# A linear-attention recurrence with MoE attention: input A without its zeros, loads one at a time, keys behind y

## The chip, the core and the metric

The kernel runs on one core of a Trainium2 chip. The metric is the device time of one execution in microseconds (us). The core's engines work through queues of their own in program order and wait for each other by semaphores: PE (TensorE: matmuls and transposes by matmul, into PSUM), DVE (VectorE), ACT (ScalarE), POOL (GpSimd) and SP, whose queue here does nothing but issue DMA loads and stores. PEld is PE's loading of weights.

## The reference, cut to what matters

```python
def _attn_ref(r, k, v, w, a, b):          # 4 batches, 8 heads, 768 steps, 40 wide
    for t in range(S):
        y[:, :, t] = np.einsum('bhd,bhde->bhe', rt, state)
        Sa = np.einsum('bhde,bhe->bhd', state, at)
        state_decay = state * wt[:, :, None, :] - np.einsum('bhd,bhe->bhde', Sa, bt)
        state = state_decay + np.einsum('bhd,bhe->bhde', vt, kt)
...
def _moe_ref(x, w_gate, wq, wk, wv, wo):  # x is y, as 4 x 768 x 320; 4 experts, the best 2 per token
        a = softmax of scale * (x @ wq[e]) @ (x @ wk[e]).T, causal
        out += weight of expert e * (a @ (x @ wv[e]) @ wo[e])
```

The recurrence over 768 steps comes first; its output y is the input of the mixture of attention experts. All is float32.

## The kernel before

**Tiling.** The 32 batch-heads are two halves s of 16, on partitions 0 to 39 and 64 to 103. The 768 steps are cut into 24 chunks of 32 steps, and the chunks into 6 windows W of 4. Within a chunk the recurrence is solved by matmuls: a triangular system is inverted once for each window (`invert`, sides P and Q on PE, fourteen elimination steps "t" on DVE), and the state ST is carried from chunk to chunk.

**Preparation of a window** (`prep`, two halves a = 0, 1 of the steps' columns, written "0x" or "1x"). Letters: w loads decay EW (into EW0), l loads EK (into KB, keys and b), e loads EA (into AB; each head's columns stand with zeros for the other half, 320 KB for one partition group). f and g are range flags on ACT, written to a scrap tile JK. a and s are scans over EW on DVE (SUF and SC), b a copy and a reciprocal between them (PC, D1P). X or x multiplies AB in place by SC (POOL or DVE, two instructions), K and H multiply the two halves of KB by SUF on POOL (two instructions each), p does K's part on DVE. m0 and m1 (`mm`) are 32 matmuls each into PSUM tile PK, read out by DVE as GB and GK and spread by POOL.

**The main loop** (24 + 1 turns n) walks the list MAIN. In a turn, each step belongs to chunk n, n-1 or n+1: g (state times AB, ACT evicts GT), f of chunk n-1 (into PF; DVE masks it to FX), t (transposed state, ACT evicts SD), k = keys of chunk n+1 (eight transposes into PK, ACT evicts LS), u (the solve, ACT evicts R), y of chunk n-1 (needs FX, SD and LS), z (DVE scales y to XT; every second chunk stores it to xT), s (state update; DVE adds it to the next ST), w (transpose of R, ACT evicts VR), v of chunk n+1. At the last chunk of a window, y's place also issues q, the gauge (rescaling by PC) of the state, and s has a gauge of its PSUM result.

**Chunk loads** are tied to steps: v loads V1 of chunk n+2, w loads R2 (VX) of n+1, y loads RX, f loads RB.

**Side work** is placed by hand: SIDE gives for each window the jobs of turns -3 to 3 relative to its first chunk (turn 4(W-1)), separated by "/" into places 0 to 9; a place k stands right behind the k-th step of MAIN. Window 1 has SIDE1 and AHEAD, window 0 has START. L258 is the DVE addition that ends side Q; it reads PK and finishes the inverse TT that u needs. Engines take all this in program order, so what stands in the list behind a waiting instruction waits with it.

**After the loop** the MoE part runs; `prepare` hangs its first loads and splits behind places 3, 5 and 7 of turns 21 to 23.

Of the kernel before, what the change touches and what calls it, by code (L numbers as in the profile page):

```python
# [21 lines left out]
NW, NC = 6, 24  # L22

SIDE = {
    -3: "0w/////0f",
    -2: "///0l1l//0g////0a0b0K0H",
    -1: "0e1e/0s0X1w///////1a1b1p",
    0: "1s1H1X////m0/1f1g////m1L",
    1: "/t14////B///t14",
    2: "/T////////P",  # L30
    3: "/////D////Q",
}
START = "x0 0w 0l 0e 1w 1l 1e x1 c0 0a 0b 0f 0g 0k 0s 0x 1a 1b 1f 1g m0 1k 1s 1x x2 m1 L B k0 t28 T D"
AHEAD = "0w 0l 1l 0e 1e 0a 0b 0f 0g 0s 0K 0H 0X 1w"

SIDE1 = {
    0: "1a1b1K1H//1s1X//m0/1f1g",
    1: "////m1/L/t4//t14",
    2: "/t10T/////B",
    3: "////P/D////Q",  # L40
}


def layouts(r, k, v, w, a, b):

    f = np.float32
    con = np.ascontiguousarray
    def em(x):
        x = x.reshape(2, 2, 8, 6, 4, 32, 40)
        return x.transpose(3, 1, 0, 6, 2, 4, 5)  # L50
    w33 = np.ones((6, 2, 2, 40, 8, 4, 33), f)
    w33[..., 1:] = em(w)
    w33[..., 0, 0] = 0
    EA = np.zeros((6, 2, 2, 40, 32, 2, 32), f)
    for s in range(2):
        EA[:, :, s, :, :, s] = em(a)[:, :, s].reshape(6, 2, 40, 32, 32)
    EK = np.stack([em(b), em(k)], 6)
    EK = EK.reshape(6, 2, 2, 40, 4, 2, 4, 2, 32).transpose(0, 1, 2, 3, 4, 6, 5, 7, 8)
    def ch(x):
        return x.reshape(2, 8, 2, 24, 32, 40)  # L60
    rr, vv = ch(r), ch(v)
    return {"EW": w33.reshape(6, 2, 2, 40, 1056), "EA": EA.reshape(6, 2, 2, 40, 2048), "EK": con(EK).reshape(6, 2, 2, 40, 2048),
            "V1": con(vv.transpose(3, 2, 0, 4, 1, 5)).reshape(24, 128, 320), "VX": con(vv.transpose(3, 2, 4, 1, 0, 5)).reshape(24, 2, 32, 640),
            "RB": con(rr.transpose(3, 0, 5, 1, 2, 4)).reshape(24, 2, 40, 512), "RX": con(rr.transpose(3, 2, 5, 1, 0, 4)).reshape(24, 2, 40, 512)}

# [17 lines left out]
def recurrence(tc, ctx, I, xT, FL, CM, early, tail=None):  # L83
    nc = tc.nc
    ep = early.enter_context(tc.tile_pool(name="early", bufs=1, side="right"))
    sp = ctx.enter_context(tc.tile_pool(name="rec", bufs=1))
    pp = ctx.enter_context(tc.tile_pool(name="rps", bufs=1, space=PSUM))
    V, A, T, PL, SY = nc.vector, nc.scalar, nc.tensor, nc.gpsimd, nc.sync
# [17 lines left out]
    O1 = MT[:, 0:512].rearrange("p (n t) -> p n t", n=32)  # L106
    DD = ring("DD", [128, 32, 16], 1, ep)[0]
    BD = ring("BD", [128, 32, 2, 32], 1, ep)[0]
    JK = ring("JK", [104, 8, 4, 32], 1, ep, BF)[0]
    TP = ring("TP", [128, 2, 56], 1, ep)[0]  # L110
    PC = ring("PC", [104, 16], 3)
    SC128 = ring("SC", [128, 64, 33], 3)
    SC = [x[0:104] for x in SC128]
    ABr = ring("AB", [104, 64, 64], 2)
    KBr = ring("KB", [128, 8, 4, 2, 64], 2)
    GB = ring("GB", [128, 32, 32], 1)[0]
    GKr = ring("GK", [128, 32, 2, 32], 2)
# [20 lines left out]
    def fill(x):  # L138
        if x == 0:
            for t in EWr:  # L140
                V.memset(t[32:64], 1.0)
            PL.memset(KBr[0][32:64], 0.0)
            PL.memset(ABr[0][32:64], 0.0)
            V.memset(d1, 0.0)
            V.memset(d1[:, ::132], 1.0)
            for t in SUFr:
                V.memset(t[:, 1056:1057], 1.0)
            V.memset(FL, 0.0)
            V.memset(D1P, 0.0)
        elif x == 1:  # L150
            PL.memset(MT, 0.0)
            PL.memset(RB, 0.0)
            PL.memset(RX, 0.0)
            PL.memset(FX, 0.0)
            PL.memset(SD, 0.0)
            PL.memset(R2, 0.0)
        else:
            V.memset(PS[32:64], 0.0)
            V.memset(PF[32:64], 0.0)
            PL.memset(D0, 0.0)  # L160
            PL.memset(BD, 0.0)
# [248 lines left out]
    inv = invert(0)  # L410
    for f in items(0, START, inv, list(inv["t"])):
        f()
    units[0]["v"]()
    for f in items(1, AHEAD, None, None) + items(0, "PQ", inv, None):
        f()
    load_c(1, 0)
    for n in range(NC + 1):
        if n == 21:
# [395 lines left out]
def body(tc, I, out):  # L814
    with ExitStack() as ctx:
# [49 lines left out]
```

## Time and profile before

| | us |
|---|---|
| median of 3 runs (lowest, highest) | 652.8 (650.13, 655.57) |
| the profiled execution | 653.06 |
| its span, first to last instruction | 651.3 |
| g of turn 1 begins | 72.59 |
| g of turn 4 begins | 115.44 |
| g of turn 20 begins | 347.61 |
| the last y is stored, MoE begins | 389.7 |

Busy shares over the whole span: PE 86%, PEld 78%, DVE 74%, ACT 53%, POOL 39%. All times in the trace count from the start of the span. A row of a timeline reads: start, duration of the group, engine, line, operation, output<-inputs, shapes, number, and in brackets the idle time before it and what ended that. L12 is line 12 of the kernel. PEclk is the granted TensorE clock as a share of full speed.

### The profile page before, as it was taken

The numbers are of one execution on the slowest core, as the hardware profiler recorded it, in microseconds if no ns is written. First come the engines' busy times: TensorE is split into PE (matmuls) and PEld (weight loads), VectorE is DVE, ScalarE is ACT, GpSimd is POOL, SyncE is SP. The second block draws the span as 40 slices with busy tenths as digits, with TensorE's granted clock in tenths as the row PEclk, the third lists the DMA queues.
The fourth block names the chain that finished last, engine by engine and source line by source line (L and its number), as shares of the span: only waits on it lengthen the run. The fifth ranks groups of instructions, "written<-read, shape, count | busy, mean of one in ns | idle before, by whom it ended". The sixth has DMA issues, their size and how long they took to land.

```text
span 651.3 us, 23336 instructions
## 1 busy us (share of the span) xinstructions
PE 557.8 (86%) x9961; PEld 510.8 (78%) x9961; DVE 482.6 (74%) x987; ACT 347.7 (53%) x726; POOL 256.0 (39%) x238
## 2 busy tenths in 40 slices
PE   0247889899799799997999987998999899999996
PEld 0247879799698799987999977887898787987784
DVE  8976597777569376856843355999998998798892
ACT  2113554354256146543543633775777687777883
POOL 7446817522450245145100023254453446233550
PEclk9857889899799689997999997998999999999998
DMA  5432236146433533551222625411311131110101
GB/s 144 128 126 69 64 104 191 30 113 166 123 84 102 136 104 85 145 175 36 81 63 73 195 64 135 111 50 56 86 46 49 34 86 54 56 26 25 62 2 66
DMA packets 42257, 57.76 MB, mean 89 GB/s; under 512 B 19809, under 2 KB 33377, under 8 KB 40225
## 3 DMA queue, kind: packets, MB, share of 16 engines
q1 hardware_dynamic: 42000, 56.05, 30.8%
q8 instruction: 80, 1.31, 0.9%
q14 instruction: 33, 0.26, 0.1%
q10 hardware_dynamic: 144, 0.13, 0.1%
HBM read 42.01 MB, written 7.86 MB: 77 GB/s over the span
## 4 chain that ended last, share of the span: by engine, by line
PE 56%; DVE 24%; issue 6%; DMA 6%; ACT 4%; POOL 1%; SPq 1%; DVEq 0%; ACTq 0%; POOLq 0%
PE pk L251 5%; PE pt L622 5%; PE pk L211 4%; PE ot L747 4%; PE pu L305 4%; PE pf L326 3%; PE sc L702 3%; PE pt L758 3%; PE ps L346 3%; PE pt L732 3%; PE pf L328 3%; DMA EW<-in_EW 3%; PE pf L314 3%; PE pg L300 3%; DVE m L712 2%
## 5 line engine op out<-in xcount | busy, mean ns | idle before, releaser
L724 POOL TENSOR_TENSOR P<-P,m 128x128 f32<-128x128 f32 (+2 forms) x96 | 89.2, 950 | 116.6 <-DVE m L720 65.9
L197 POOL TENSOR_TENSOR KB<-KB,SUF 104x512 f32<-104x512 f32 x32 | 45.6, 1453 | 107.7 <-DVE SUF L184 81.6
L713 ACT ACTIVATE P<-sc,m 128x128 f32<-128x128 f32 (+2 forms) x96 | 60.8, 634 | 26.3 <-DVE m L712 13.7
L747 PE MATMUL ot<-pt,vv 128*128 128x256 f32 (+1 forms) x384 | 61.2, 292 | 6.1 <-DVE ots L753 5.4
L702 PE MATMUL sc<-ks,qs 128*128 128x384 f32 (+4 forms) x256 | 62.7, 347 | 2.8 <-ACT P L713 1.9
L736 DVE TENSOR_TENSOR pt<-pt,pt 128x384 fp32r<-128x384 f32 (+1 forms) x96 | 58.9, 618 | 5.3 <-ACT pt L735 3.6
L317 DVE TENSOR_TENSOR FX<-pf,CM 64x512 f32<-64x512 f32 x48 | 32.7, 682 | 37.1 <-PE pf L314 36.7
L747 PEld LDWEIGHTS ot<-pt,vv 128*128 128x128 f32 x384 | 51.4, 191 | 10.4 <-DVE ots L753 8.1
L712 DVE TENSOR_REDUCE m<-sc 128x1 f32<-128x128 f32 (+2 forms) x96 | 58.7, 615 | 1.0 <-PE sc L705 0.4
L735 ACT ACTIVATE pt<-pt 128x384 fp32r<-128x384 f32 (+1 forms) x96 | 52.0, 543 | 10.5 <-PE pt L732 9.0
L193 POOL TENSOR_TENSOR AB<-AB,SC 40x1024 f32<-40x1024 f32 x20 | 44.3, 2216 | 32.9 <-DVE SC L189 13.7
L732 PE MATMUL pt<-CM,P 128*128 128x128 f32 x336 | 52.9, 274 | 3.9 <-DVE qs L631 2.6
L211 PE MATMUL pk<-KB,AB 104*64 104x64 f32 x768 | 29.3, 244 | 29.9 <-DVE AB L193 29.9
L302 ACT ACTIVATE GT<-pg,CM 128x320 f32<-128x320 f32 x48 | 22.7, 523 | 60.0 <-PE pg L300 60.0
L211 PEld LDWEIGHTS pk<-KB,AB 104*64 104x64 f32 x768 | 27.5, 157 | 31.3 <-issue 20.0
L326 PE MATMUL pf<-FX,LS 128*40 128x64 f32 x768 | 46.7, 222 | 1.5 <-DVE FX L317 1.3
L622 PE MATMUL pt<-xh,wq 128*128 128x384 f32 x192 | 42.9, 358 | 4.2 <-DVE qs L631 4.0
L702 PEld LDWEIGHTS sc<-ks,qs 128*128 128x128 f32 x256 | 40.7, 191 | 6.6 <-ACT P L713 6.0
L328 PE MATMUL pf<-RX,SD 80*40 80x64 f32 x736 | 44.9, 220 | 0.0
L326 PEld LDWEIGHTS pf<-FX,LS 128*40 128x40 f32 x768 | 41.0, 116 | 4.4 <-DVE FX L317 3.2
L311 ACT ACTIVATE VR<-pu 80x1024 f32<-80x1024 f32 x24 | 24.5, 1020 | 34.9 <-PE pu L310 34.8
L307 ACT ACTIVATE R<-pu 32x640 f32<-32x640 f32 x48 | 33.3, 693 | 18.3 <-PE pu L305 17.7
(146 smaller groups left out, 1403.8 us busy)
## 6 DMA issues: line engine op xcount, KB each, us to landing
KB<-in_EK SPq DMA_DIRECT2D x24, 320.0 KB
AB<-in_EA SPq DMA_DIRECT2D x24, 320.0 KB
ks<-ks SPq DMA_DIRECT2D x32, 192.0 KB
V<-in_V SPq DMA_DIRECT2D x24, 160.0 KB
R<-in_VX SPq DMA_DIRECT2D x48, 80.0 KB
RX<-in_RX SPq DMA_DIRECT2D x48, 80.0 KB
RB<-in_RB SPq DMA_DIRECT2D x48, 80.0 KB
xT<-XT SPq DMA_DIRECT2D x24, 160.0 KB
```

Of the source, the lines that this page charges most:

```text
L211: T.matmul(PK[rows(t, 64), x // 2, y:y + 64], ab[:, n], kb[0:104, 4 * a + x, c, t], start=True, stop=True)
L326: T.matmul(pf[rows(r), x], ls[:, x, r], FX[:, :, x, r], start=True, stop=c == 0)
L328: T.matmul(pf[rows(r), x], SD[:, x, r], RX[:, :, x, r], start=False, stop=True)
L622: T.matmul(p, w, x, start=(j == 0), stop=(j == len(prs) - 1))
L702: T.matmul(ps[:, c, 0:cw], QS[b][:, e, o], KS[b][:, e, z, k], start=(z == 0), stop=(z == 1 and not last), skip_group_check=True)
L712: V.tensor_reduce(m[:, 0, t:t + 1], ps[:, 0:ch, 0:cw], axis=AX.XY, op=OP.max, negate=True)
L713: later(DE, lambda: A.activation(pv, ps[:, 0:ch, 0:cw], AF.Exp, bias=m[:, 0, t:t + 1], accum_out=m[:, 1, t:t + 1]))
L724: PL.tensor_tensor(P[:, 0:n], P[:, 0:n], m[:, 3, t:t + 1].to_broadcast([128, n]), op=OP.mult)
L732: T.transpose(p[:, 128 * y:128 * y + 128], st["P"][t][:, 128 * c:128 * c + 128], ident)
L735: A.activation(h, p[:, 0:n], AF.Copy)
L736: later(DL, lambda: V.tensor_tensor(l, p[:, 0:n], f32(h), op=OP.subtract))
L747: T.matmul(po[:, 128:256] if one else po, VV[b][:, k, e].rearrange("p a b -> p (a b)"), PT[:, 256 * k:256 * k + (128 if one else 256)], st ...
```

## The change

1. EA comes without zeros: half the bytes, into a buffer of its own for one half (EAr; at window 0 the second half lies in the still unused GK1). The product X reads that buffer and writes AB, whose zeros come from memsets over the whole tile. One buffer serves both halves, so 1e must follow 0X.
2. Loads l are split: l is the first partition group, u the second. The big loads stand at separate places: 0w and 0e in turn -3, 0l in turn -2, and in turn -1 1w and 0u (place 0), 1l, 1e and 1u.
3. In MAIN, k stands behind z instead of ahead of u. LS has two buffers instead of three. Flags write GB instead of JK.
4. Scan 0s moves to the end of turn -2, 1a and 1b to place 1 of turn -1 (from place 8), 1s to place 8 of turn -1 (from turn 0), 1p to turn 0 (from turn -1); flags, m0, B and D move to fit. In SIDE1 m1 moves behind y.

```diff
 SIDE = {
-    -3: "0w/////0f",
-    -2: "///0l1l//0g////0a0b0K0H",
-    -1: "0e1e/0s0X1w///////1a1b1p",
-    0: "1s1H1X////m0/1f1g////m1L",
-    1: "/t14////B///t14",
+    -3: "/0w///0e",
+    -2: "//////0l//0f0g/0a0b0s",
+    -1: "1w0u0X0K0H/1a1b///1l/1e///1f1g1s1u1X",
+    0: "1p1H///m0//////m1L",
+    1: "/t14//B/////t14",
     2: "/T////////P",
-    3: "/////D////Q",
+    3: "///D//////Q",
 }
-START = "x0 0w 0l 0e 1w 1l 1e x1 c0 0a 0b 0f 0g 0k 0s 0x 1a 1b 1f 1g m0 1k 1s 1x x2 m1 L B k0 t28 T D"
-AHEAD = "0w 0l 1l 0e 1e 0a 0b 0f 0g 0s 0K 0H 0X 1w"
+START = "x0 0w 0l0u 0e 1w 1l1u 1e x1 c0 0a 0b 0f 0g 0k 0s 0x 1a 1b 1f 1g m0 1k 1s 1x x2 m1 L B k0 t28 T D"
+AHEAD = "0w 0l0u 1l1u 0e 0a 0b 0f 0g 0s 0K 0H 0X 1w 1e"
 
 SIDE1 = {
-    0: "1a1b1K1H//1s1X//m0/1f1g",
-    1: "////m1/L/t4//t14",
-    2: "/t10T/////B",
-    3: "////P/D////Q",
+    0: "1a1b1K1H/1f1g/1s1X/m0",
+    1: "////m1L/t4//t14",
+    2: "/t10T//B",
+    3: "///P///D///Q",
 }
...
-    EA = np.zeros((6, 2, 2, 40, 32, 2, 32), f)
-    for s in range(2):
-        EA[:, :, s, :, :, s] = em(a)[:, :, s].reshape(6, 2, 40, 32, 32)
...
-"EA": EA.reshape(6, 2, 2, 40, 2048)
+"EA": con(em(a)).reshape(6, 2, 2, 40, 1024)
...
-    JK = ring("JK", [104, 8, 4, 32], 1, ep, BF)[0]
+    EAr = ring("EA", [104, 32, 32], 1, ep)[0]
...
-    LSr = ring("LS", [128, 8, 2, 40], 3)
+    LSr = ring("LS", [128, 8, 2, 40], 2)
...
+    EAr = EAr, GKr[1].rearrange("p n r t -> p (n r t)")[0:104, 0:1024].rearrange("p (n t) -> p n t", t=32)
...
-            PL.memset(ABr[0][32:64], 0.0)
+            PL.memset(ABr[0], 0.0)
...
-                e.tensor_tensor(x, x, sc[rows(s), :, 0:32], op=OP.mult)
+                e.tensor_tensor(x, ea[rows(s)], sc[rows(s), :, 0:32], op=OP.mult)
...
-            A.activation(JK, EW.rearrange("p (h n c) -> p h n c", n=4, c=33)[:, :, :, 1:33], AF.Relu, bias=CM[0:104, 192 + x:193 + x],
+            A.activation(GB[0:104].rearrange("p (h n) c -> p h n c", n=4), EW.rearrange("p (h n c) -> p h n c", n=4, c=33)[:, :, :, 1:33], AF.Relu, bias=CM[0:104, 192 + x:193 + x],
...
-    MAIN = [("g", 0), ("f", -1), ("t", -1), ("k", 1), ("u", 0), ("y", -1), ("z", -1), ("s", 0), ("w", 0), ("v", 1)]
+    MAIN = [("g", 0), ("f", -1), ("t", -1), ("u", 0), ("y", -1), ("z", -1), ("k", 1), ("s", 0), ("w", 0), ("v", 1)]
```

## Rows read from the trace of the kernel before

**Rows 1.** The page: busy engines, and PE's instruction queue (packets, MB, share).

```profile
PE 557.8 (86%) x9961; PEld 510.8 (78%) x9961; DVE 482.6 (74%) x987; ACT 347.7 (53%) x726; POOL 256.0 (39%) x238
...
q8 instruction: 80, 1.31, 0.9%
```

**Rows 2.** Busy time by stretch: length, PE, PEld, DVE, ACT, POOL, PEclk, DMA, GB/s.

```profile
98.38:133.62 35.24, 32.13 (x896) 30.57 (x898) 23.50 (x23) 13.81 (x21) 20.89 (x12) 0.95 0.42 113
...
115.44:133.62 18.18, 15.07 (x388) 14.07 (x386) 12.28 (x13) 7.24 (x11) 9.31 (x6) 0.91 0.18 42
...
133.62:157.35 23.73, 23.05 (x646) 21.75 (x642) 20.92 (x44) 13.22 (x20) 4.33 (x6) 1.00 0.47 125
157.35:191.93 34.58, 29.82 (x773) 28.31 (x771) 19.53 (x20) 13.89 (x21) 16.56 (x11) 0.90 0.43 111
178.61:191.93 13.32, 13.32 (x389) 12.77 (x387) 8.57 (x10) 7.20 (x11) 7.63 (x5) 1.00 0.23 59
191.93:221.27 29.34, 24.62 (x647) 23.19 (x643) 20.89 (x44) 13.22 (x20) 7.15 (x8) 0.94 0.47 123
...
221.27:252.60 31.33, 31.33 (x769) 29.77 (x770) 19.42 (x20) 13.93 (x21) 14.11 (x8) 0.84 0.36 102
...
276.31:310.65 34.34, 29.51 (x772) 27.84 (x771) 19.50 (x20) 13.93 (x21) 16.91 (x11) 0.90 0.38 108
...
334.38:347.61 13.23, 13.23 (x388) 12.70 (x385) 4.55 (x6) 6.69 (x10) 0.00 (x0) 1.00 0.23 67
```

**Rows 3.** Waits of PE, 95 to 350: us in total, times, longest.

```profile
PE pk L282 <- DVE TT L258: 6.7, 2, 3.6
PE pk L251 <- issue: 5.3, 2, 4.1
PE pu L310 <- issue: 4.7, 1, 4.7
```

**Rows 4.** The chain that ended last, turns 3 and 4: start, us, what.

```profile
105.68 9.24 DMA EW<-in_EW
...
117.73 3.10 DVE KB L197 x2
```

**Rows 5.** Timeline of SP and DVE: the first load of EW and its scan.

```profile
1.99 0.79 SPq L175 DMA_DIRECT2D EW<-in_EW  x2
...
5.79 2.36 DVE L184 TENSOR_TENSOR_SCAN SUF<-EW,D 104x1056 f32<-104x1056 f32 x1 [0.77 <-DMA EW<-in_EW]
```

**Rows 6.** Timelines of DVE and POOL: alone and beside each other.

```profile
12.15 2.48 DVE L197 TENSOR_TENSOR KB<-KB,SUF 104x512 f32<-104x512 f32 x4
...
60.46 4.41 POOL L193 TENSOR_TENSOR AB<-AB,SC 40x1024 f32<-40x1024 f32 x2
...
63.49 3.59 DVE L184 TENSOR_TENSOR_SCAN SUF<-EW,D 104x1056 f32<-104x1056 f32 x1
...
105.21 1.74 DVE L337 TENSOR_TENSOR ST<-ST,PC 104x640 f32<-104x640 f32 x1
...
110.28 0.83 DVE L337 TENSOR_TENSOR ps<-ps,PC 104x640 f32<-104x640 f32 x1 [0.48 <-PE ps L346]
...
155.56 4.65 POOL L197 TENSOR_TENSOR KB<-KB,SUF 104x512 f32<-104x512 f32 x4 [17.70 <-DVE SUF L184]
```

**Rows 7.** Timeline of PE, turn 8: y begins.

```profile
185.32 0.31 PE L326 MATMUL pf<-FX,LS 128*40 128x64 f32 x4
```

**Rows 8.** Timelines of DVE and PE, turn 6: FX, and y behind it.

```profile
147.41 1.38 DVE L317 TENSOR_TENSOR FX<-pf,CM 64x512 f32<-64x512 f32 x2
...
148.85 0.36 PE L326 MATMUL pf<-FX,LS 128*40 128x64 f32 x3 [0.22 <-DVE FX L317]
```

**Rows 9.** Timelines of DVE, PE and POOL, turns 0 and 1.

```profile
71.13 0.70 DVE L214 STREAM_TRANSPOSE GK<-pk 128x512 f32<-128x512 f32 x1
...
72.59 0.61 PE L300 MATMUL pg<-ST,AB 104*64 104x40 f32 x14 [2.04 <-DVE ST L355]
...
73.87 4.41 POOL L193 TENSOR_TENSOR AB<-AB,SC 40x1024 f32<-40x1024 f32 x2
```

More of the change, by code (lines that the diff above doesn't have):

```diff
@@ L61, in layouts @@
     rr, vv = ch(r), ch(v)
-    return {"EW": w33.reshape(6, 2, 2, 40, 1056), "EA": EA.reshape(6, 2, 2, 40, 2048), "EK": con(EK).reshape(6, 2, 2, 40, 2048),
+    return {"EW": w33.reshape(6, 2, 2, 40, 1056), "EA": con(em(a)).reshape(6, 2, 2, 40, 1024), "EK": con(EK).reshape(6, 2, 2, 40, 2048),
             "V1": con(vv.transpose(3, 2, 0, 4, 1, 5)).reshape(24, 128, 320), "VX": con(vv.transpose(3, 2, 4, 1, 0, 5)).reshape(24, 2, 32, 640),
@@ L161, in fill @@
             PL.memset(BD, 0.0)
-            PL.memset(ABr[1][32:64], 0.0)
+            PL.memset(ABr[1], 0.0)
             PL.memset(KBr[1][32:64], 0.0)
@@ L170, in prep, with load @@
         EW, SUF, sc, ab, kb = EWr[a if w == 0 else 0], SUFr[a], SC[w % 3][:, half], ABr[w % 2][:, half], KBr[w % 2][:, 4 * a:4 * a + 4]
-        pc = PC[w % 3][:, 8 * a:8 * a + 8]
+        pc, ea = PC[w % 3][:, 8 * a:8 * a + 8], EAr[a if w == 0 else 0]
         sv = SUF[:, 1:1057].rearrange("p (n c) -> p n c", c=33)
-        def load(t, src):
-            for s in two:
+        def load(t, src, which=two):
+            for s in which:
                 SY.dma_start(t[rows(s)], I[src][w, a, s])
-        def load_a():
-            for s in two:
-                SY.dma_start(flat(ab[rows(s)]), I["EA"][w, a, s])
         def flag(x):
             i = 2 * w + a
-            A.activation(JK, EW.rearrange("p (h n c) -> p h n c", n=4, c=33)[:, :, :, 1:33], AF.Relu, bias=CM[0:104, 192 + x:193 + x],
+            A.activation(GB[0:104].rearrange("p (h n) c -> p h n c", n=4), EW.rearrange("p (h n c) -> p h n c", n=4, c=33)[:, :, :, 1:33], AF.Relu, bias=CM[0:104, 192 + x:193 + x],
                          scale=1.0 - 2.0 * x, accum_out=FL[0:104, 2 * i + x:2 * i + x + 1])
@@ L197, in kmul @@
                 e.tensor_tensor(x, x, sv[:, :, 1:33].rearrange("p (x t c) n -> p x t c n", t=2, c=4)[:, :, t], op=OP.mult)
-        return dict(w=lambda: load(EW, "EW"), e=load_a, l=lambda: load(kb.rearrange("p x c t n -> p (x c t n)"), "EK"),
+        return dict(w=lambda: load(EW, "EW"), e=lambda: load(flat(ea), "EA"),
+                    l=lambda: load(kb.rearrange("p x c t n -> p (x c t n)"), "EK", (0,)),
+                    u=lambda: load(kb.rearrange("p x c t n -> p (x c t n)"), "EK", (1,)),
                     f=lambda: flag(0), g=lambda: flag(1), a=suf, b=per, s=pre, x=lambda: amul(V), X=lambda: amul(PL),
@@ L282, in keys @@
             T.transpose(PK[:, x // 4, 128 * (x % 4):128 * (x % 4) + 104], kb[0:104, x, cw].rearrange("p t n -> p (t n)"), ident[0:104, 0:104])
-        A.activation(LSr[c % 3], gaps(PK), AF.Copy)
+        A.activation(LSr[c % 2], gaps(PK), AF.Copy)
     def chunk(c):
@@ L287, in chunk @@
         ab, gk, tt = ABr[w % 2], GKr[w % 2], TTr[w % 2]
-        ls, r2 = LSr[c % 3], R2
+        ls, r2 = LSr[c % 2], R2
         st0, st1, xt = STr[c % 2], STr[(c + 1) % 2], XT
@@ L839, in body @@
                 moe(tc, c4, I, xT, out, CM[:, 0:128], pre[0])
-_INS = {"EW": (6, 2, 2, 40, 1056), "EA": (6, 2, 2, 40, 2048), "EK": (6, 2, 2, 40, 2048), "V1": (24, 128, 320), "VX": (24, 2, 32, 640), "RB": (24, 2, 40, 512),
+_INS = {"EW": (6, 2, 2, 40, 1056), "EA": (6, 2, 2, 40, 1024), "EK": (6, 2, 2, 40, 2048), "V1": (24, 128, 320), "VX": (24, 2, 32, 640), "RB": (24, 2, 40, 512),
         "RX": (24, 2, 40, 512), "CM": (128, 261),
```

## The prediction

> **What bounds the kernel now.** I read the page first: PE is busy 86% of the span, more than any other engine [rows 1], so time is lost where PE stands still or runs slowly. Then I cut the trace at the starts of step g (L300), one turn n of the main loop each, and joined the turns in pairs [rows 2]. A turn with n mod 4 = 0 carries both halves of mm, mod 1 nothing large, mod 2 side P, mod 3 side Q. The reader should see that equal pairs differ: mod 1 + 2 takes 23.73 us (three of the four pairs, from 23.71), but 29.34 at n=9; mod 3 + 0 takes 31.3 to 35.2. An undisturbed turn takes 13.32 (n=8) or 13.23 (n=19).
>
> The waits of PE over these turns show two causes [rows 3]. One is "issue", a stall for nothing the profile shows: 4.7 us in step w (n=7), 4.1 in side P (n=10), and 1.25, the rest of the 5.3, in side Q (n=15). All three fall into dense transfers: their pairs move 108 to 123 GB/s, turn 8, which has none, 59 [rows 2]. PE's instructions come by DMA too, in 80 pieces of 16 KB [rows 1]; I infer that pieces came late behind data. The other cause is L258, waited for 3.1 and 3.6 us. At n=3, half EW of 1w is issued at 105.35, behind four EA loads, and takes 9.24 us; scan 1a waits on DVE, and 1b, 1p and L258 stand behind it [rows 4], and behind L258 the keys on PE, since both use PK. After each stall the granted clock is low (0.84 in the pair from n=11) [rows 2].
>
> **The change, part by part.**
>
> *EA halved, loads spread.* By the shapes a chunk loads 640 KB in each turn, a half of EW is 330, of EK 640, of EA 640 before and 320 after. Turn mod 2 falls from 1,280 EK + 640 + 320 of xT = 2,240 KB to 1,280. Turn mod 3 keeps 2,250: 1,280 EA + 330 EW + 640 before, 960 EK + 330 EW + 320 EA + 640 after, but with half as much waiting at once. So the stall of n=10 goes, and pairs mod 1 + 2 all cost 23.73. In mod 3 a stall may stay (0 to the 4.7 of n=7, four times over), but PE will wait for DVE there anyway, as follows; I take 1.0 in all, ends 0 and 8.5.
>
> *1w at the head of its turn.* 0s moves behind 0a and 0b, where PE does side P, and ends 0.6 us after g of mod 3. The kernel's first EW, with nothing ahead of it, let its scan start 3.8 us after its issue [rows 5]. So EW is there at 4.4, and the 9.24 us of n=3 are gone.
>
> *What DVE and POOL do to each other.* This decides, as 0X, 0K, 0H, 1X and 1p now run in this pair. Beside POOL's second AB product, which ends at 64.87, scan 1a starts at 63.49 and takes 3.59 rather than 2.36: it ran after that end. The gauge of the state takes 1.74 beside POOL's products, while the gauge of ps, of the same size but from PSUM, takes 0.83 beside POOL's AB. 1p's two products, 0.62 each where POOL reads nothing, take 3.10 beside POOL's KB products, some 1.16 each [rows 4 to 6]. So with both operands in SBUF, one engine waits out the other's instruction and they alternate; with an operand in PSUM DVE is not held. The Trainium skill, "SBUF — State Buffer", section on the two sides of SBUF, says the same, an exclusive lock for a whole instruction; by it the pair below holds, while with 3.10 for 1p whatever POOL does the sum would be that of rival B.
>
> From g of mod 3, in us: 0X on POOL 0.6 to 5.0 (two of 2.2). 1a 5.0 to 7.4. POOL's first product of 0K (1.16) to 8.5, 1b (0.4) to 8.9, POOL's second to 9.8, gauge of the state (0.83) to 10.7, first of 0H to 11.8; XT, gauge of ps and the state's sum (three of 0.83 at most, from PSUM, the first as soon as y is done) to 13.1; second of 0H to 13.0; 1s 13.1 to 15.4. PE's next g is at 13.3, undelayed. L258 now stands behind 1s, 15.4 to 16.1, and u, due at 16.1, just finds it. But 1X starts when 1s ends: first half to 17.6, 1p's first product to 18.2, second half of 1X to 20.4, 1p's second to 21.0, FX to 22.4. y was due at 19.2: in turn 8 it began 6.7 us after g with the keys ahead of it [rows 7], so 5.9 without them. PE stands 3.2 us. The rest of the turn (13.32 - 6.7 and the keys' 0.85) ends at 29.9. Before, an equal wait (3.1) made turn 4 cost 18.18 instead of 13.32 [rows 2], 1.75 more than the wait, for the clock; that makes the pair 31.7. At n=3 DVE is busy until g comes (its steps t fill turn 2), so 0s ends 4.9 us after g rather than 0.6, and PE has P and Q in the turn: 36.1 there. Against 35.24 + 34.58 + 31.33 + 34.34 = 135.5 stand 36.1 + 3 x 31.7 = 131.2: -4.3. Bounds: -19 if 1p and FX make y wait for nothing, +11 if EW lands 1 us late and the clock costs twice as much.
>
> *Keys behind y.* PE's work stays, but keys (0.88) filled its wait for FX. In turn 6 FX stands behind fourteen steps t on DVE and ends at 148.79; y starts at 148.85 after a wait of 0.22 [rows 8]. Now u ends 0.85 earlier, y still waits, and keys follow: +0.85. Pairs mod 1 + 2: 4 x (23.73 + 0.85) = 98.3, against 23.73 + 29.34 + 23.71 + 23.73 = 100.5: -2.2.
>
> *Keys behind m0 at n=0.* Keys write PK, which GB and GK must have read; these stand behind 1s on DVE, GK ends at 71.83. Before, keys came ahead of m0 and waited for none of that [rows 9]. Now PE is through with m0 at 67.0 (POOL's AB ends at 64.87) and stands 4.9 us. Keys, s, w, v follow, partly at low clock, 5.5 us in all: g at 77.4, not 72.59. Part comes back, as m1 of n=1 waited for POOL until 78.28 [rows 9]; now it comes 4.5 us after g, at 81.9. Net +3.6, ends 0 and 6.3.
>
> *Edits at no cost.* AB's product reads EA instead of itself, same size. AB's memsets cover more partitions in the same length. Flags write GB while it is dead, and run behind VR, where ACT has no other work until P or Q ends. LS needs two buffers, as y has read the old one when keys write. B and D still follow R on ACT. On SP, V1 now stands behind 1e, which waits for POOL's 64.87; the late keys cover it, else 1 us. The tail and the MoE keep their instructions.
>
> **Sum.** The profiled execution took 653.06 (span 651.3) and the median is 652.8, so nothing is shifted. 653.06 - 4.3 - 2.2 + 3.6 + 1.0 = 651.2: the old waits go, and y waiting for FX takes their place.
>
> **Rivals.**
>
> *B. 1p gets through.* If it takes 3.10, as beside shorter products, FX ends at 20.6 and y waits 1.4, little more than the 1.25 of n=15, after which the clock stayed up. The pair costs 29.9 - 1.8 = 28.1: 651.2 - 4 x 3.6 = 637. For it: the order of DVE and POOL is not seen beside AB products. Against: the scan at 63.49.
>
> *C. EW still lands late.* Its turn still holds 2,250 KB. From a landing 5.0 us after g on, each us goes through to 1s, 1p and y. At 9.24 from the issue, 4.8 us too late: 651.2 + 4 x 4.8 = 670, slower. For it: n=3, 7 and 15 took so long. Against: 1w now goes out ahead of the other loads.
>
> *D. The stalls stay.* If crowding was not their cause, n=10 keeps its 5.6, and n=7 its 4.7 and the low clock (some 8 in all) less the 3.2 that y's wait absorbs: 651.2 - 1.0 + 5.6 + 4.8 = 661, slower. For it: n=6 and 14 carry the loads of n=10 without a stall. Against: no turn with little traffic has one. The Trainium skill, "DMA: Bandwidth & Descriptors", section on queues, rings and completion order, says a DMA engine goes round its rings packet by packet; by that an instruction piece would not stand behind a backlog, which is this rival. The dense stretches around all three stalls speak against it.
>
> **Chances.** The forecast 0.52 (its own range 645 to 658), B 0.28, D 0.14, C 0.06. About 1% (6.5 us) is what a measurement of this kernel can tell. Faster: B and the forecast's lower edge, 0.30. Slower: C and D, 0.20. The same: 0.50. The range goes from 633, a little below B, to 661, D; C is left out.
>
> **What would show it.** Right: waits of PE for FX of some 3 us at y in turns 4, 8, 12 and 16, with the clock down behind them; no wait for L258 before keys, no DVE wait for EW over 2 us; keys at n=0 some 5 us late; "issue" gone from mod 2. Wrong: no such wait at y (B), DVE waiting for EW in mod 3 (C), "issue" waits of 4 us (D).

## The result, and the profile after

The changed kernel takes 647.05 us (median; 641.82 to 653.51), the kernel before 652.09 beside it: a ratio of 0.9915, 95% interval 0.9890 to 0.9939. That is 5 us, 0.85%, less. The profiled execution took 647.44, its span 645.6 (before 651.3). Forecast were 651.2, with 645 to 658 as the range of the likeliest case. Medians here and below are of all runs, while ratios leave out runs over 1.5% above the fastest of the same kernel, so the two can differ.

First the windows, by pair of turns as in [rows 2]: length, busy time of PE, PEld, DVE, ACT, POOL, PEclk, DMA share, GB/s. The first four lines are pairs mod 3 + 0, the last two pairs mod 1 + 2.

```profile
100.74:136.87 36.13, 34.38 (x896) 32.34 (x898) 24.62 (x23) 14.78 (x23) 19.19 (x12) 0.91 0.48 116
161.60:191.56 29.96, 27.57 (x772) 25.71 (x770) 20.16 (x20) 13.81 (x21) 19.15 (x12) 1.00 0.44 116
216.32:247.32 31.00, 28.90 (x772) 27.01 (x770) 20.92 (x20) 13.81 (x21) 19.13 (x12) 0.94 0.44 115
272.06:302.56 30.50, 28.69 (x771) 27.07 (x770) 20.04 (x20) 13.81 (x21) 19.38 (x12) 0.94 0.43 110
136.87:161.60 24.73, 23.53 (x646) 21.85 (x642) 22.51 (x45) 13.22 (x20) 2.54 (x4) 1.00 0.41 113
191.56:216.32 24.76, 23.54 (x646) 21.84 (x642) 22.54 (x45) 13.22 (x20) 2.55 (x4) 1.00 0.39 105
```

The pairs mod 3 + 0 give 7.9 us back (135.5 to 127.6). The pair from n=9, 29.34 before, takes 24.76 like its equals, and each of those has become a whole us longer.

The waits, 95 to 350, as in [rows 3] (us in total, times, longest):

```profile
DVE SUF L179 <- DMA EW<-in_EW: 7.6, 4, 3.4
PE pf L323 <- DVE FX L314: 6.9, 9, 2.1
...
DVE KB L192 <- DMA KB<-in_EK: 5.0, 3, 2.3
PE ps L319 <- issue: 1.8, 1, 1.8
PE pu L302 <- issue: 1.7, 1, 1.7
PE pk L248 <- issue: 1.7, 1, 1.7
...
PE pu L307 <- issue: 0.7, 1, 0.7
```

The wait of the keys for the addition that ends side Q (L258, now L255) is gone, and so are pauses of 4 us. In their place stand y's wait for FX (0.5 to 0.8 in each turn mod 1 and mod 2, 2.1 in turn 12), a wait of 1p for EK, and four short pauses of PE, which all stand in turns mod 3 and mod 0.

Timelines of the kernel after (start, duration, engine, line, operation, shapes, in brackets the idle time before it), DVE, POOL and PE: the keys at n=0, two pauses of turn 7, and turn 12, whose g starts at 229.83.

```profile
70.19 1.65 PE L279 MATMUL pk<-CM,KB 104*128 104x104 f32 x8 [4.85 <-DVE GK L211]
...
170.83 0.53 PE L307 MATMUL pu<-CM,R 64*80 64x64 f32 x11 [0.71 <-issue]
...
176.58 1.46 PE L248 MATMUL pk<-MT,BD 64*64 64x64 f32 x44 [1.69 <-issue]
...
228.93 2.35 DVE L184 TENSOR_TENSOR_SCAN SC<-EW,D1P 104x1056 f32<-104x1056 f32 x1
231.20 0.66 DVE L255 TENSOR_TENSOR TT<-TT,pk 128x512 f32<-128x512 f32 x1
232.89 3.85 DVE L192 TENSOR_TENSOR KB<-KB,SUF 104x512 f32<-104x512 f32 x2 [1.03 <-DMA KB<-in_EK]
236.66 1.38 DVE L314 TENSOR_TENSOR FX<-pf,CM 64x512 f32<-64x512 f32 x2
...
231.42 4.77 POOL L188 TENSOR_TENSOR AB<-EA,SC 40x1024 f32<-40x1024 f32 x2 [2.51 <-DVE SC L184]
...
233.91 2.08 PE L208 MATMUL pk<-KB,AB 104*64 104x64 f32 x64
238.09 0.36 PE L323 MATMUL pf<-FX,LS 128*40 128x64 f32 x3 [2.10 <-DVE FX L314]
240.89 1.65 PE L279 MATMUL pk<-CM,KB 104*128 104x104 f32 x8
```

Turn 12 is the forecast's picture: 1s, L255, 1p, FX stand in one queue on DVE, 1p is stretched to 3.85 beside POOL's 1X, PE is through with m0 at 235.99 and waits until 238.09, and the keys behind it run at low clock (1.65 instead of 0.93).

### The profile page after: what moved, and what is told of

Same layout as the page of the kernel before. It is cut to its first block, busy times and chain, and to the rows that moved or that the text cites. A ratio compares the mean times of both kernels' runs of the same rounds, so it can differ in the third digit from the quotient of the medians.

```text
span 645.6 us, 23340 instructions
## 1 busy us (share of the span) xinstructions
PE 555.9 (86%) x9961; PEld 504.7 (78%) x9961; DVE 488.5 (76%) x987; ACT 347.3 (54%) x726; POOL 256.0 (40%) x238
## 4 chain that ended last, share of the span: by engine, by line
PE 54%; DVE 28%; issue 6%; ACT 4%; DMA 4%; SPq 0%; DVEq 0%; ACTq 0%
PE pk L248 6%; PE pt L619 5%; PE ot L744 4%; PE pf L323 4%; PE ps L343 3%; PE pk L208 3%; PE sc L699 3%; PE pt L755 3%; PE pf L325 3%; PE pt L729 3%; DVE TP L230 3%; DVE MT L232 3%; PE pg L293 3%; DVE m L709 3%; PE pk L279 3%
## 5 line engine op out<-in xcount | busy, mean ns | idle before, releaser
L188 POOL TENSOR_TENSOR AB<-EA,SC 40x1024 f32<-40x1024 f32 x20 | 44.5, 2224 | 93.9 <-DVE SC L184 74.2
L732 ACT ACTIVATE pt<-pt 128x384 fp32r<-128x384 f32 (+1 forms) x96 | 52.0, 543 | 10.5 <-PE pt L729 9.0
L323 PEld LDWEIGHTS pf<-FX,LS 128*40 128x40 f32 x768 | 42.3, 118 | 12.4 <-DVE FX L314 11.4
L619 PE MATMUL pt<-xh,wq 128*128 128x384 f32 x192 | 42.9, 359 | 4.4 <-DVE qs L628 4.2
L213 POOL TENSOR_TENSOR GK<-GK,CM 128x512 f32<-128x512 f32 x24 | 27.1, 1128 | 46.6 <-DVE GK L211 45.5
```

The lines of the kernel that those rows point to most:

```text
L323: T.matmul(pf[rows(r), x], ls[:, x, r], FX[:, :, x, r], start=True, stop=c == 0)
L619: T.matmul(p, w, x, start=(j == 0), stop=(j == len(prs) - 1))
L732: A.activation(h, p[:, 0:n], AF.Copy)
```

## The experiments

Times are medians; ratios are to the kernel before, run beside each.

| kernel | us (lowest, highest) | ratio, 95% interval |
|---|---|---|
| the kernel after | 647.05 (641.82, 653.51) | 0.9915, 0.9890 to 0.9939 |
| after, k ahead of u | 642.13 (633.41, 647.69) | 0.9779, 0.9708 to 0.9849 |
| after, 1p behind FX | 647.13 (640.99, 648.72) | 0.9889, 0.9836 to 0.9941 |
| after, k ahead, 1p behind FX | 631.54 (626.07, 645.92) | 0.9621, 0.9571 to 0.9671 |
| after, k ahead, 1K on POOL | 631.89 (625.01, 639.57) | 0.9666, 0.9617 to 0.9714 |
| the same, late EK | 628.28 (625.61, 633.96) | 0.9652, 0.9600 to 0.9705 |
| the same, and idle bytes | 647.40 (643.56, 653.24) | 0.9892, 0.9843 to 0.9942 |
| before, new loads, 1p late | 645.97 (639.99, 648.47) | 0.9887, 0.9837 to 0.9936 |
| after, without 1X and 1H | 639.07 (634.96, 642.58) | 0.9816, 0.9725 to 0.9908 |
| after, early 1u | 647.65 (644.07, 652.78) | 0.9967, 0.9921 to 1.0014 |

Lengths of turns in their profiled executions, from start of g to start of g (turn 5 + 6 is a pair mod 1 + 2; turn 20 has no side work):

| kernel | 4 | 7 | 8 | 10 | 12 | 16 | 5 + 6 | 20 |
|---|---|---|---|---|---|---|---|---|
| before | 18.18 | 21.26 | 13.32 | 19.23 | 13.51 | 19.60 | 23.73 | 9.51 |
| after | 17.23 | 16.37 | 13.59 | 14.11 | 17.49 | 16.99 | 24.73 | 9.80 |
| after, second trace | 15.40 | 18.61 | 16.77 | 14.12 | 16.03 | 18.65 | 24.73 | 9.79 |
| k ahead | 16.82 | 19.10 | 16.87 | 13.59 | 17.01 | 16.98 | 23.71 | 9.51 |
| 1p behind FX | 14.95 | 15.66 | 16.67 | 14.11 | 14.19 | 17.58 | 24.74 | 9.79 |
| k ahead, 1p behind FX (an execution of 642.05) | 16.83 | 17.61 | 17.54 | 13.59 | 16.44 | 18.02 | 23.68 | 9.51 |
| k ahead, 1K on POOL (an execution of 639.57) | 14.53 | 18.02 | 16.80 | 13.58 | 13.75 | 17.75 | 23.68 | 9.51 |
| k ahead, 1K, late EK | 14.80 | 14.76 | 13.31 | 13.59 | 13.46 | 13.45 | 23.69 | 9.52 |
| and idle bytes | 17.46 | 16.84 | 17.62 | 13.58 | 19.24 | 16.86 | 26.83 | 9.52 |
| before, new loads, 1p late | 19.59 | 14.68 | 19.59 | 13.60 | 18.53 | 16.90 | 23.72 | 9.51 |
| without 1X, 1H | 14.94 | 16.98 | 16.71 | 14.11 | 13.60 | 15.71 | 24.73 | 9.80 |
| early 1u | 14.77 | 17.17 | 16.69 | 14.12 | 16.23 | 16.72 | 24.75 | 9.80 |

**What the keys behind y cost.**

```diff
-    MAIN = [("g", 0), ("f", -1), ("t", -1), ("u", 0), ("y", -1), ("z", -1), ("k", 1), ("s", 0), ("w", 0), ("v", 1)]
+    MAIN = [("g", 0), ("f", -1), ("t", -1), ("k", 1), ("u", 0), ("y", -1), ("z", -1), ("s", 0), ("w", 0), ("v", 1)]
```

> The kernel after with k back ahead of u and LS in three buffers; all loads, scans and side work stay where they are. My theory: the new place of k costs 2.4 us at n=0 (g of turn 1 came 3.67 later, of turn 2 still 2.40), 1.0 us in each pair of turns mod 1 + 2 (24.75 against 23.73) and 0.3 us in each turn without side work, while y's wait for FX stays unless k's 0.85 us fill it. So about 2.4 + 4.0 + 1.5 = 8 us faster than the kernel after: 639. Rival: k now waits for the DVE addition that ends side Q (L255), which stands behind 1s; in turn 12 it ended at 231.86, 2.0 us after g, and PE gets to k at 2.4, so a wait of up to 0.5 is possible, and if 1s is late by 2 us more in turn 4 or 16 the gain there is gone: 643 to 647, with waits of PE for L255 ahead of k.

It took 642.13, by the medians 5 us less than the kernel after and by the ratios, whose intervals don't meet, 9, where 8 were expected. The trace has the three prices of the move one by one: g of turn 3 comes at 98.02 instead of 100.74, each pair mod 1 + 2 takes 23.70 instead of 24.75 (4.2 in all), turns 19 to 22 give 0.28 each. The wait for L255 that the rival feared is 0.9 once, ahead of turn 1, and not in turns 4 to 16. Of these 8 us 2.8 went back in the traced execution in the pairs mod 3 + 0, where the pair from n=7 took 35.97 for 29.96: side Q paused for 3.6 us instead of 1.69, and turn 8, in which PE waits for nothing, ran at a clock of 0.77. That need not be the move's doing: in a second trace of the kernel after (below) the same pause is 3.34 and the pair takes 35.38. Windows of the kernel with k ahead, turns 7 and 8:

```profile
155.61:174.71 19.10, 14.76 (x389) 14.03 (x385) 12.00 (x11) 9.07 (x14) 13.18 (x8) 0.94 0.55 138
174.71:191.58 16.87, 16.87 (x386) 16.14 (x387) 7.09 (x9) 4.76 (x7) 6.23 (x5) 0.77 0.19 46
```

The mirror image, k alone moved in the kernel before:

> The kernel before with k moved behind z and nothing else (side work keeps its place among the other steps). My theory: the move costs by itself what the kernel after shows: 2.4 to 3.7 us at n=0, 0.5 to 0.85 in each turn mod 1 and mod 2 (4 to 7 in all) and 0.3 in each turn without side work, some 8 to 10 us: 660 to 662. The two waits of 3 us for L258 ahead of k turn into waits of u for it. Rival: the order of PE's own work is no cost, since PE has the same instructions; then 652, and the kernel after lost its gain elsewhere.

It gave 686.41, and this time tells nothing of the question: 0l and 1l now stood ahead of the last keys that read the same buffer, so keys of one chunk per window waited for that load (25.4 us in 8 waits) and used its data. The turns that this leaves alone do show the price of the move: turn 5 takes 10.62 for 10.13, turn 19 13.51 for 13.23 and turn 20 9.79 for 9.51, as in the kernel after.

**What the loads alone bring.** A first form, with 0l and 0u in turn mod 2 and 1e directly behind 1w, had the same fault:

> The kernel before with the loads of the change alone: EA without its zeros through one buffer, EK in two parts at separate places (0l and 0u in turn mod 2, 1l and 1u in mod 3), 0e a turn earlier; scans, products and the order of the steps stay, and with them PE's instruction stream. My theory: the pauses called issue (4.7 us in step w of turn 7, 4.1 in side P of turn 10, 1.25 in side Q of turn 15) come from instruction pieces that wait behind dense transfers, and the lateness of EW in turns 3, 7 and 15 from the four EA loads ahead of it; both go. Turn 10 takes 14.1 instead of 19.7, the pair from n=7 gives 5 to 8 back, those from n=3 and n=15 some 5 each: 632 to 637. Rival 1: the pauses belong to places in PE's instruction stream, whatever is loaded; then they stand at the same three places and only EW's lateness goes: 643 to 645. Rival 2: EW is late because its own transfer is slow; then only the pauses go, and 640 or so is left.

It took 659.62 (ratio 1.0110): besides the keys' waits for EK (5.0 us), 1e waited in SP's queue for POOL's 0X and held up RX, R and V behind it. The form that answers the question:

```diff
-    -3: "0w/////0f",
-    -2: "///0l1l//0g////0a0b0K0H",
-    -1: "0e1e/0s0X1w///////1a1b1p",
+    -3: "0w////0e/0f",
+    -2: "///0l//0u0g////0a0b0K0H",
+    -1: "/0s0X1w/1l1u////1e///1a1b1p",
```

> The kernel before with the loads alone changed, in a form that leaves the keys' data intact: EA without zeros through one buffer (0e in turn mod 1, 1e behind 0X), 0l and 0u at places 3 and 5 of turn mod 2, 1l and 1u at place 2 of turn mod 3 behind 1w. (In the earlier kernel of this kind, and in the one with k alone moved, a part of EK was loaded over keys of the window before that were still to be read: PE's keys waited for that load, 25 us in all in the latter, so their times tell nothing of the change.) Scans, products, the order of the steps and PE's instruction stream are those of the kernel before. My theory: turn 10 takes 14 instead of 19.2 us without its pause; EW is no longer late at n=3 and 15, so the two waits of over 3 us for L258 go; turn 7 keeps at most 2.5 of its 4.7: 632 to 640. Rival 1 (pauses belong to the instruction stream): issue of 4 us stays in turns 7 and 10, 643 to 646. Rival 2 (EW is slow by itself): the L258 waits stay.

645.97, 6 us less than before. It is not the loads alone, though: by a slip of mine 1a, 1b and 1p stand at place 9 instead of 8, behind the addition that ends side Q (L256 here; in the first form too). DVE's timeline, turn 8 (its g starts at 175.18):

```profile
175.35 0.69 DVE L256 TENSOR_TENSOR TT<-TT,pk 128x512 f32<-128x512 f32 x1 [5.11 <-PE pk L249]
175.96 2.35 DVE L180 TENSOR_TENSOR_SCAN SUF<-EW,D 104x1056 f32<-104x1056 f32 x1
...
178.67 3.11 DVE L193 TENSOR_TENSOR KB<-KB,SUF 104x512 f32<-104x512 f32 x2
181.71 2.35 DVE L185 TENSOR_TENSOR_SCAN SC<-EW,D1P 104x1056 f32<-104x1056 f32 x1
183.97 1.36 DVE L315 TENSOR_TENSOR FX<-pf,CM 64x512 f32<-64x512 f32 x2
```

So the addition waits for nothing any more, but both scans and 1p stand ahead of FX, and y waits. Waits of PE, 95 to 350:

```profile
PE pf L324 <- DVE FX L315: 12.4, 8, 3.3
...
PE ps L320 <- issue: 1.7, 1, 1.7
PE pk L249 <- issue: 1.1, 1, 1.1
```

What the slip doesn't touch can be read. Turn 10 has lost its pause (13.60 for 19.23, 5.6 us, the larger part of the gain), and on PE's unchanged stream the pauses of turn 7 fell from 4.7 to 1.1, so rival 1 is out as far as one trace of each kernel can tell. What the earlier EW brings by itself, and what the moved scans bring beyond the loads, stays open; both together, without the keys' move, are the kernel with k ahead of u (642).

**What makes y wait.** Four edits of the kernel after. First 1p a place later, behind FX on DVE:

```diff
-    0: "1p1H///m0//////m1L",
+    0: "1H/1p//m0//////m1L",
```

> The kernel after with one job moved: 1p from place 0 to place 1 of its turn, so that DVE takes FX before 1p. My theory: y's wait for FX in turns 4, 12 and 16 (2.1 us at the longest, 8.1 in all) comes from 1p standing ahead of FX while it alternates with POOL's 1X; without it y starts when m0 ends, the clock stays up, and each of these turns takes some 14 instead of 17 us: 6 to 9 us faster than the kernel after, 638 to 641. Rival: the products of DVE and POOL take their time anyway; GB and GK stand behind 1p instead, and k, which writes the same PSUM tile, waits for GK: no gain (645 to 648), with waits of PE for GK ahead of k in turns 4, 12 and 16.

The wait in turn 12 went (the longest left is 0.7 us), the rival's wait of k for GK is 0.5 once, turns 4 and 12 took 14.95 and 14.19, and yet the time was 647.13: turns 3, 8 and 16 came out 0.6 to 3.1 us longer, around pauses of 1.95 in side Q of turn 7 and 2.41 at t of turn 16. Then the products beside 1p, left out:

```diff
-    -1: "1w0u0X0K0H/1a1b///1l/1e///1f1g1s1u1X",
-    0: "1p1H///m0//////m1L",
+    -1: "1w0u0X0K0H/1a1b///1l/1e///1f1g1s1u",
+    0: "1p///m0//////m1L",
```

> The kernel after with POOL's products 1X and 1H left out from window 2 on (AB and half of KB then hold old numbers for the second half of the columns; PE, DVE and ACT do all they did). It takes away what 1p alternates with and leaves the rest: 1s, L255 and the wait for EK stand ahead of 1p as before. Theory 1 (1p and POOL take turns, as the forecast said): 1p's two products take 1.24 instead of 3.3 to 3.9 us, FX ends ahead of m0, and y in turn 12 waits for nothing instead of 2.10; turn 12 takes some 14 instead of 17.49, turns 4 and 16 lose up to 1 us: 641 to 644. Theory 2 (1p is long for a reason of its own): it keeps 3 us and more, and y its wait.

Turn 12 fell to 13.60. The time was 639.07, but the interval of its ratio overlaps that of the kernel after, so it is turn 12 that shows the effect. DVE's timeline there:

```profile
232.33 0.66 DVE L255 TENSOR_TENSOR TT<-TT,pk 128x512 f32<-128x512 f32 x1
233.79 1.29 DVE L192 TENSOR_TENSOR KB<-KB,SUF 104x512 f32<-104x512 f32 x2 [0.81 <-DMA RB<-in_RB]
235.01 1.39 DVE L314 TENSOR_TENSOR FX<-pf,CM 64x512 f32<-64x512 f32 x2
```

And 1u earlier, so that EK is there in time:

```diff
-    -1: "1w0u0X0K0H/1a1b///1l/1e///1f1g1s1u1X",
+    -1: "1w0u0X0K0H/1a1b///1l1u/1e///1f1g1s1X",
```

> The kernel after with 1u moved from place 8 to place 4 of its turn, beside 1l, so that all of EK is there when L255 ends. 1p then waits for nothing (it waited 2.31, 1.03 and 1.61 us for EK in turns 4, 12 and 16). Theory 1 (what holds 1p is POOL's 1X): 1p starts earlier and takes as much longer, its first product behind 1X's first, its second behind 1X's second; in turn 12 it ends 4.9 us after L255 as before, and y's wait of 2.1 stays: 646 to 648. Theory 2 (the late EK sets it): 1p ends 1.0 to 2.3 us earlier, y's wait in turn 12 falls to 1.1 or less: 643 to 645. PE's pauses in turn 7 may grow, since turn mod 3 has its loads closer together.

647.65. Timelines of DVE, POOL and PE, turn 12:

```profile
232.93 0.66 DVE L255 TENSOR_TENSOR TT<-TT,pk 128x512 f32<-128x512 f32 x1
233.51 4.96 DVE L192 TENSOR_TENSOR KB<-KB,SUF 104x512 f32<-104x512 f32 x2
238.39 1.38 DVE L314 TENSOR_TENSOR FX<-pf,CM 64x512 f32<-64x512 f32 x2
...
233.14 4.78 POOL L188 TENSOR_TENSOR AB<-EA,SC 40x1024 f32<-40x1024 f32 x2 [2.35 <-DVE SC L184]
...
239.83 0.36 PE L323 MATMUL pf<-FX,LS 128*40 128x64 f32 x3 [2.36 <-DVE FX L314]
```

The same two products take 1.29 with nothing beside them, 3.85 when they come late, and 4.96 when they come early: 1p ends 4.9 us after L255 either way (236.74 - 231.86; 238.47 - 233.59). So in turn 12 POOL's product sets the end of 1p, not EK; in turn 4, where EK was 2.31 us late, the earlier load takes 1.2 us off that end, and the time doesn't show it. So 1p's length beside 1X, on which the forecast hung, is shown.

A second trace of the unchanged kernel after:

> The kernel after once more, for a second trace of it. My theory: the pauses stand at the same places of PE's stream (u of turn 4, w and side Q of turn 7, t or u of turn 16), with other lengths; y's wait for FX of some 2 us shows in turn 12, and in turns 4, 8 and 16 only where PE had not paused ahead of it. Pairs of turns mod 1 + 2 take 24.7 again. Rival: the pauses stand elsewhere, and what the first trace shows is chance.

The execution took 650.88. Pauses came again in u of turn 4 (1.14), side Q of turn 7 (3.34) and t of turn 16 (2.29), in w of turn 7 only 0.2; y's longest wait was 2.2, in turn 12 again, and pairs mod 1 + 2 were 24.7. Their places stay, their lengths don't.

**The two moves together.** k ahead of u, and 1p behind FX, or 1p's products on POOL:

```diff
-    0: "1p1H///m0//////m1L",
+    0: "1H/1p///m0/////m1L",
...
+    0: "1K1H////m0/////m1L",
```

> Both moves at once: the kernel after with k back ahead of u, and 1p one place later, so that DVE takes FX before 1p. With k ahead alone turns 4, 12 and 16 took 16.82, 17.01 and 16.98 us, of which y's wait for FX was up to 2.0 and the low clock behind it the rest. My theory (1p ahead of FX makes y wait): these three turns fall to some 14.2, as turns 4 and 12 did to 14.95 and 14.19 when 1p alone was moved: 642 - 8 = 634. Rival: the time of DVE and POOL comes back elsewhere, as moving 1p alone gave 647.1 against 647.05 in sum: turns 3, 8 and 16 become longer by as much, and 642 is left.

> The kernel after with k back ahead of u, and the two products of 1p computed by POOL (1K) ahead of 1H: DVE has none of them, and nothing on DVE with both operands in SBUF is left beside 1X. m1, which needs them, comes 12 us after g. My theory (DVE is held by POOL's products through 1p): FX follows f at once in turns 4, 8, 12 and 16, y never waits for it, and these turns take some 14 us where the clock is up: 632 to 636, as good as moving 1p behind FX or a little better. If y's wait came from something else than 1p, it stays: 640 or more. Against it: 1H ends some 2.3 us later, and if EK of 1u lands late, m1 waits for POOL (a wait of PE for KB at the end of the turn).

631.54 and 631.89, some 20 us below the kernel before and 15 below the one after. Either answer to 1p brings this. But alone, behind later keys, the move of 1p was worth nothing by the medians, and here 10 us. The traces don't say why: the executions that they show took 642.05 and 639.57, 10.5 and 7.7 above these medians. In them y's waits for FX are gone (0.2 us at most), but PE pauses for 8.2 and 6.8 us in all, and with 1p behind FX turns 4, 12 and 16 take 16.4 to 18.0 there, not the expected 14.2.

**Are the pauses late instructions?** Each pause called issue ends shortly after a packet of the instruction queue (q8, 16 KB): in all 14 traces, between 95 and 350, there are 48 such pauses, and every one ends 2.4 to 3.0 us after such a packet began and 1.3 to 1.8 after it had landed. Transfers of the kernel before in 215.50 to 215.75 and 167.75 to 168.00 (packets, MB, share of 16 engines; a packet is counted where it begins):

```profile
q8 instruction: 1, 0.02, 33.8%
...
q8 instruction: 1, 0.02, 29.3%
```

33.8% of 16 engines in 0.25 us is 1.35 us. PE went on at 218.39 and 170.68, both times 2.6 to 2.9 us after that packet began:

```profile
170.68 0.86 PE L310 MATMUL pu<-CM,R 64*80 64x64 f32 x11 [4.71 <-issue]
...
218.39 0.90 PE L251 MATMUL pk<-TT,BD 64*64 64x64 f32 x12 [4.06 <-issue]
```

In the kernel after, such packets begin at 168.00 to 168.25 and 174.00 to 174.25, and PE goes on at 170.83 and 176.58. In turn 10 the packet begins 13.5 us after g in the kernel before, and 8.5 to 8.8 after g in the kernel before with new loads, whose PE stream is the same: at least 4.7 us earlier, and there is no pause. The Trainium skill, "Runtime: NRT & Kernel Launch", section on the mechanics of instruction fetch, says that engines fetch their code in 16 KB blocks of their own accord and that crossing a block is mostly hidden; these rows agree with the 16 KB, and in dense stretches not with "mostly hidden".

Two kernels were to show the dose. Late EK, from the kernel with 1K on POOL:

```diff
-    -1: "1w0u0X0K0H/1a1b////1l/1e//1f1g1s1u1X",
-    0: "1K1H////m0/////m1L",
+    -1: "1w0u0X0K0H/1a1b////1e///1f1g1s1X",
+    0: "1l1u1K1H////m0/////m1L",
```

> The kernel with 1K on POOL, and 1l and 1u (640 KB) loaded a turn later, behind g of turn mod 0. Turn mod 3 then carries 1,610 KB instead of 2,250, turn mod 0 1,280 instead of 640; PE's instruction stream is the same as in the kernel with 1K on POOL. My theory (PE stands because instruction pieces come late behind dense transfers): the pauses of turn 7, in step w and side Q (4.3 us in sum with k ahead, 2.4 in the kernel after), are gone or under 1 us, turn 7 takes 13.3 to 14, turn 8 14 at full clock: 5 to 8 us less than with 1K alone, 626 to 630. Rival: the pauses belong to those places of PE's instruction stream whatever is loaded beside them; then turn 7 keeps 2 to 4 us of issue and the time is that of 1K alone. A second way to fail: the pauses move to turn mod 0, where the loads now are.

Its profiled execution looks like the theory (turns 7 and 8 at 14.76 and 13.31, pauses of 0.5 and 0.6 in turn 7 and of 1.1 in turn 4), but 628.28 is no clear gain over 631.89: the intervals of the ratios nearly coincide. And the edit did less than its text says. Nothing that SP's queue waits for holds these loads back until turn 8; they went out at 163.40, in turn 7, and the turn still moved 2.49 MB. Then bytes that nobody reads:

```diff
-    -1: "1w0u0X0K0H/1a1b////1e///1f1g1s1X",
+    -1: "1w0u0X0K0H/1a1b/1l1u///1e/1l1u//1f1g1s1X",
```

> The kernel with 1K on POOL and late EK, and 1l and 1u issued twice more in turn mod 3, at places 2 and 6, into the part of KB that the real ones overwrite: 1,280 KB that nobody reads. PE's instruction stream, the products and the scans are the same. In the traces so far every pause called issue ends some 1.5 to 1.9 us after a packet of the instruction queue (16 KB) started to land plus its own 1.2 us, and in turn 10 of the kernel before that packet started 13.2 us after g, in the kernels with EK spread 8.2 to 8.7. Theory (crowding): the added bytes make the pieces of turns 7, 11 or 15 start later by several us; issue in turns 7 and 8 together goes from 1.07 us to 4 or more, and with the low clock behind it the time is 6 to 15 us above that of the kernel it starts from (628): 634 to 643. Rival (the pieces don't suffer from data): pauses as there, time within 2 us. Beside it EW, RX or RB may land later, which would show as waits of DVE for EW or of PE for RX, and not as issue.

647.40: 19 us more, above the expected 6 to 15. Waits of PE, 95 to 350, without and with the idle bytes:

```profile
PE pu L302 <- issue: 1.1, 1, 1.1
...
PE pk L248 <- issue: 0.6, 1, 0.6
PE pu L307 <- issue: 0.5, 1, 0.5
```

```profile
PE pk L208 <- POOL KB L192: 6.0, 4, 2.9
PE pk L248 <- issue: 4.5, 2, 2.8
PE ps L319 <- issue: 1.8, 1, 1.8
...
PE pf L323 <- issue: 0.6, 1, 0.6
PE pu L307 <- issue: 0.2, 1, 0.2
```

Pauses grow from 2.2 to 7.1 us, more than the two traces of the kernel after differ (5.9 and 7.0). Turn 8, in which PE waits for nothing, takes 17.62 for 13.31. The packet ahead of the pause in side Q of turn 7 begins 12.7 us after g where it began 10.9 without the idle bytes, and the pause is 2.8 for 0.6. So dense transfers do make instruction pieces late. Not all of the 19 us is that: the real EK is later too, and m waits for POOL (6.0, in turns 4 and 12).

## Why the prediction was right, and where it was off

Forecast and measured, from the starts of g:

| term | forecast | measured |
|---|---|---|
| pairs mod 3 + 0, with the rest of their stalls | -4.3 + 1.0 | 127.6 - 135.5 = -7.9 |
| pairs mod 1 + 2 | -2.2 | 99.0 - 100.5 = -1.5 |
| up to g of turn 3 (keys at n=0) | +3.6 | 100.74 - 98.38 = +2.4 |
| turns 19 to 22 | 0 | 42.9 - 41.8 = +1.1 |
| sum | -1.9 | -5.9 (spans: -5.7) |

The four terms missed by -4.6, +0.7, -1.2 and +1.1 us, by -4.0 in all; that the last three all but cancel is luck.

**Right: the chain on DVE.** Counted from g of turn 11 (216.32), 1s starts at 12.6 (forecast 13.1), L255 ends at 15.5 (16.1), 1p 4.9 later (4.9), FX ends at 21.7 (22.4), and y was due at 19.7 (19.2). So the wait is 2.1 instead of 3.2. Its whole price, 17.49 against 13.60 in the same kernel without 1X and 1H, is 3.9: 2.1 of wait and 1.8 behind it, the 1.75 that the forecast took over from turn 4. 1p did not get through (rival B): POOL and DVE alternate, as [rows 6] had shown for other products. The Trainium skill, "SBUF — State Buffer", section on the two sides of SBUF, says that a DVE instruction with two inputs in SBUF and a POOL instruction that reads SBUF lock each other out, each for its whole length. By that lock 1p must come out so, and the trace agrees: 4.96 against 1.29.

**Off: how often it shows.** The term "pairs mod 3 + 0" charged 3.2 plus 1.75 to each of turns 4, 8, 12 and 16. In the profiled execution only turn 12 paid it. In turns 4 and 16 PE paused for instructions by 1.7 and 1.8 ahead of y, and in turn 8 it had lost 2.4 in turn 7, so FX was there. The pauses did not add 1.0 on top; they took the place of y's wait. So the pairs from n=7, 11 and 15 cost 3.6 less than forecast and the 1.0 did not come: this is the 4.6 by which the term missed. It holds for this one execution. In the second trace the same four pairs take 132.9, almost the forecast 132.2, but not for the forecast reason: y waits over 1 us in turn 12 alone again, and 7.0 us of pauses with a low clock behind them (0.79 in turn 8) make up the amount. A hit of this term would be luck. The prediction's remark that the clock is low after each stall is also too wide: after the pause of turn 15 in the kernel before it stayed at 1.00 until the next g.

**Right: EW and its rival C.** 1w goes out 0.83 after g of turn 7, and scan 1a starts 5.3 after g (forecast 4.4 to 5.0). DVE's waits for EW are 1.8 us at most there and later; turn 3 alone has 3.4, because 0s ends 5.1 after its g, as the forecast had it for that turn (4.9). That the pair from n=3 took 36.13, forecast 36.1, is luck: y did not wait in turn 4, PE paused there.

**Right: the stall of turn 10 goes (rival D's other side).** Turn 10 has no pause in any trace with EK spread. For turn 7 the forecast's "0 to 4.7" held 2.4.

**Keys behind y: right in mechanism, two sizes off.** In pairs mod 1 + 2 y waits for FX and keys follow it, but in both turns, by 0.5 each (10.62 for 10.14, 14.11 for 13.59), where the step had put 0.85 into the second alone: the term is -1.5 for -2.2. The same 0.5 shows in the kernel before with k alone moved. At n=0 keys waited 4.85 us for GK, as worked out (4.9), and ran at low clock (1.65). But GK ended at 70.13 instead of 71.83, so g of turn 1 came at 76.26 instead of 77.4; what came back by turn 3 was 1.3, forecast 1.2. In the second trace keys waited only 1.49 there, because PE had waited 2.97 for POOL ahead of m0. The assumption that the tail costs nothing was wrong: without any wait a turn takes 9.80 for 9.51, and 9.51 again with k ahead.

## What to carry to other kernels

Before you move an instruction of DVE or POOL, look at which of the other's instructions with operands in SBUF lie beside it: two short products took 1.29 us alone and 4.96 beside two long ones, and whatever stands behind them pays. Try two moves together even where one of them brings nothing alone: by the medians k ahead of u brought 5 us, 1p behind FX nothing, both 15, though no trace here shows why. A load's place in a list fixes its time only if something ahead of it in the queue waits.

## What the runs showed of the hardware that I had not expected

A pause of PE can cost as much again behind it: after 3.6 us in side Q, PE worked through the next turn without a wait at a granted clock of 0.77, 16.87 us for 13.31. After pauses of 1.7 and 0.7 in turn 7 of the kernel after the clock stayed at 1.00. But after 1.7 in turn 4 and 1.8 in turn 16 of the same execution it was 0.86 and 0.87 over the rest of the turn, and after y's wait of 2.1 in turn 12 it was 0.82. So the length of a pause alone does not tell its price.

The order of PE's steps has a price without any wait. In turn 20, from start to start, t takes 0.74 us with k behind it and 0.84 with u; y takes 1.84 with s behind it and 1.97 with k; k takes 0.81 ahead of u and 0.86 ahead of s. Together that is the 0.28 us of a turn of 9.5.
